# Attention and bilinear feed-forward on one core: the last out products as seven half products for eight

## The chip, the core and the metric

The kernel runs on one core of a Trainium2 chip: TensorE (matmuls into PSUM), VectorE, ScalarE, GpSimd (SBUF alone in this kernel), SyncE (SP), which issues most transfers, and 16 DMA engines. The metric is device time of one execution in microseconds; lower is better.

## The reference

Attention with a forget gate over 8 batches, 8 heads, 576 tokens and a head size of 64; its output, 4608 tokens of 512, goes through a bilinear feed-forward of 1536 features.

```python
scores = scale * np.matmul(q, k.transpose(0, 1, 3, 2))
log_f = np.log(np.clip(f, 0.0001, 1.0))
cum = np.cumsum(log_f, axis=-1)
decay = cum[:, :, :, None] - cum[:, :, None, :]
scores = np.where(causal, -1000000000.0, scores + decay)
attn = softmax(scores)
x = (attn @ v).transpose(0, 2, 1, 3).reshape(B * S, H * D)
out = ((x @ w_a) * (x @ w_b)) @ w_out
```

(softmax stands for the three lines that write it out.)

## The kernel before

Attention runs over 32 pairs of heads (pr, t). The feed-forward follows behind the batches that are ready: for a piece of 256 to 512 tokens (`cuts`) TensorE makes psa and psb, ScalarE copies psa to fp16 (a16), VectorE multiplies it by psb into the hidden tiles ht (line 1072), and the out step multiplies ht by w_out into pso, 12 feature blocks of 128 for each block of 128 tokens.

A product on TensorE is issued in two halves by `mm_halves` (line 74): 64 stationary columns each, on both halves of the array, over the same moving columns. The two run beside each other, and the text calls them a pair.

The last 1024 tokens are two halves of 512, which start at `TW` = (3584, 4096). Their hidden values come from `winograd`: x of the two halves and w_a, w_b are taken as 2 by 2 blocks, and for each of 12 feature blocks fb seven products (`product`, m 1 to 7, four matmuls of 512 columns each) stand for the eight plain ones. It needs differences of weights (`sub_w`, line 1218, named xT or wb after the buffers that they reuse) and of x (`add_x`, line 1224), fp16 on VectorE. The products gather in PSUM in wg and wb; `snap` copies stages of them to SBUF (wu, wv; ScalarE or VectorE), `combine` (line 1273) adds: c11, c12 and c22, and multiplies: h1 (first half's hidden values, on GpSimd, into hy or ht) and h2 (second half's, on VectorE, into hx). For odd fb c22 runs on GpSimd too (wv<-wv).

`out_step` then makes eight blocks of 128 tokens, 12 pairs of 512 columns each, a ScalarE copy to osb and a store by SP. The last block is cut into 256, 128 and 128 columns (`last_out`, `last_copy`, `last_store`: psz, half), and its middle piece is stored from ScalarE's queue.

What runs when is not decided at run time. Every step is an `Op` with dependencies; a planner outside the file laid them out, and its result stands in it as tables: ORDER (the sequence in which all Ops are issued), CHOICE (the engine, where there is one) and SLOTS (which buffer of each ring a tile gets). Each engine works through its own part of ORDER one instruction after another and waits at semaphores; a late instruction holds everything behind it on its engine.

```python
PLAIN = range(0, 12, 2)
for tb in range(8):
    out_step(TW[0], tb, muls[tb // 4], 0.04 * TW[0])
order = laid_out()
for o in order:
    o.fn(o.eng)
```

## Time and profile before

| | us |
|---|---|
| median of 3 runs | 396.08 |
| lowest, highest | 394.84, 400.15 |
| profiled execution, device time | 395.96 |
| its span, first to last instruction | 393.9 |

The busy shares by slice (40 slices of 9.85 us, tenths of busy time) show where each engine works:

```profile
PE   7899999999999999999999999999999989999997
DVE  7888898998997779788887798758998898989700
ACT  4998999999888878778988588789898662455221
POOL 8699677778877689884897779678976980357600
```

PE is TensorE, DVE VectorE, ACT ScalarE, POOL GpSimd. Attention and feed-forward share the slices up to the 33rd; the hidden stage of the last 1024 tokens fills slices 34 to 37, and their out step the last two.

### The profile page before, as it was taken

Reading aid. Unit: us, or ns where it says so; the run is one execution under the profiler, and the core shown is the slowest. Engines: PE = TensorE matmul, PEld = TensorE weight load, DVE = VectorE, ACT = ScalarE, POOL = GpSimd, SP = SyncE. Lnnn points to the kernel's source line nnn. Section 1 sums busy time; section 2 is a strip of 40 time slices with the busy share of each in tenths; the row PEclk is TensorE's granted clock in tenths of the full one; section 3 lists DMA queues with packets and bytes.
Section 4 is the critical chain, followed back from the end, with each engine's and each line's share of the span. In section 5 each row is a group of like instructions: output and inputs, shape, how many; then the busy total and the mean of one; then the engine's idle time right before and its main releaser. Section 6 shows DMA issues by size and latency. Waiting matters only on the chain.

```text
span 393.9 us, 14686 instructions
## 1 busy us (share of the span) xinstructions
PE 382.3 (97%) x5720; PEld 251.3 (64%) x5720; DVE 319.2 (81%) x1015; ACT 296.5 (75%) x817; POOL 280.4 (71%) x482
## 2 busy tenths in 40 slices
PE   7899999999999999999999999999999989999997
PEld 3557977969766665655555665555655677666665
DVE  7888898998997779788887798758998898989700
ACT  4998999999888878778988588789898662455221
POOL 8699677778877689884897779678976980357600
PEclk9999999999999999999999999999999999999999
DMA  7999999999999999999999999999999895100022
GB/s 125 265 188 173 153 147 232 231 289 284 188 233 245 219 285 211 263 236 266 256 229 264 256 227 213 260 270 229 207 203 223 185 139 137 55 1 2 2 108 107
DMA packets 147365, 76.87 MB, mean 195 GB/s; under 512 B 124384, under 2 KB 128352, under 8 KB 147296
## 3 DMA queue, kind: packets, MB, share of 16 engines
q1 hardware_dynamic: 132856, 68.72, 77.2%
q0 software_dynamic: 14256, 7.08, 14.6%
q8 instruction: 44, 0.72, 0.7%
q14 instruction: 25, 0.20, 0.2%
q10 hardware_dynamic: 184, 0.14, 0.1%
HBM read 52.05 MB, written 9.58 MB: 156 GB/s over the span
## 4 chain that ended last, share of the span: by engine, by line
PE 79%; DMA 7%; POOL 4%; DVE 4%; ACT 3%; issue 2%; DVEq 0%; ACTq 0%; POOLq 0%
PE pso L74 20%; PE psa L74 16%; PE psb L74 15%; PE wg L74 5%; PE wb L74 4%; PE sc L550 3%; PE pvx L768 3%; DMA PTB<-PB 2%; PE psT L358 2%; DMA wout<-in_moe_w_out_dram 2%; POOL PA L725 2%; PE sc L538 2%; ACT PA L704 2%; PE wake L74 2%; DVE S L673 2%
## 5 line engine op out<-in xcount | busy, mean ns | idle before, releaser
L673 DVE CUSTOM_DVE_ANT_0 S<-sc,spread 64x576 f32<-64x576 f32 (+4 forms) x232 | 125.4, 561 | 14.2 <-ACT PA L704 4.8
L725 POOL TENSOR_SCALAR PA<-PA,st 128x256 f16<-128x256 f16 (+2 forms) x180 | 85.6, 487 | 10.5 <-DVE st L714 7.5
L74 PE MATMUL psa<-xT,wa 128*64 128x512 f16 (+2 forms) x864 | 88.9, 333 | 1.7 <-DVE ht L1072 1.7
L74 PE MATMUL psb<-xT,wb 128*64 128x512 f16 (+2 forms) x864 | 88.7, 332 | 0.4 <-DVE ht L1072 0.2
L704 ACT ACTIVATE PA<-S,st 128x256 f16<-128x256 f32 (+2 forms) x168 | 84.1, 503 | 6.2 <-DVE st L673 5.7
L74 PE MATMUL pso<-wout,ht 128*64 128x512 f16 x696 | 85.5, 380 | 0.3 <-DMA wout<-in_moe_w_out_dram 0.3
L725 POOL TENSOR_SCALAR PB<-PB,st 128x512 f16<-128x512 f16 (+1 forms) x90 | 64.0, 719 | 23.4 <-DVE st L714 8.7
L74 PEld LDWEIGHTS <-wa 128*64 128x64 f16 x960 | 55.4, 110 | 26.3 <-issue 4.2
L74 PEld LDWEIGHTS <-wb 128*64 128x64 f16 x960 | 56.5, 110 | 24.3 <-issue 1.7
L288 ACT CAST a<-psa 128x512 f16<-128x512 f32 (+1 forms) x90 | 49.4, 551 | 18.1 <-PE psa L74 14.9
L1072 DVE TENSOR_TENSOR ht<-psb,a 128x512 f16<-128x512 f32 (+1 forms) x90 | 57.6, 649 | 6.2 <-PE psb L74 4.1
L74 PEld LDWEIGHTS <-ht 128*64 128x64 f16 x696 | 38.8, 110 | 27.9 <-issue 2.6
L704 ACT ACTIVATE PB<-S,st 128x512 f16<-128x512 f32 x56 | 40.2, 720 | 3.4 <-DVE st L673 2.9
L704 ACT ACTIVATION_READ_ACCUMULATOR PA<-S,st 128x1 f32 x168 | 31.9, 190 | 0.0
L700 ACT ACTIVATE PB<-S,st 128x576 f16<-128x576 f32 x28 | 21.7, 776 | 9.2 <-DMA PTB<-PB 3.6
L630 POOL TENSOR_SCALAR_AFFINE_SELECT spread<-spread 128x768 f32<-128x768 f32 x24 | 20.9, 871 | 10.7 <-DMA spread<-cum_d 10.3
L288 ACT COPY osb<-pso 128x512 f32<-128x512 f32 x28 | 16.3, 583 | 15.4 <-PE pso L74 15.4
L768 PEld LDWEIGHTS <-nv 128*64 128x64 f16 x640 | 22.0, 110 | 6.7 <-DMA PTA<-PA 2.1
L1273 POOL TENSOR_TENSOR hy<-wu 128x512 f16<-128x512 f32 x9 | 11.4, 1278 | 20.3 <-DVE wu L1273 20.3
L673 DVE CUSTOM_DVE_ANT_1 S<-sc,spread 128x256 f32<-128x256 f32 x48 | 19.7, 420 | 6.5 <-PE sc L538 1.9
L714 DVE RECIPROCAL st<-st 128x2 f32<-128x2 f32 x128 | 18.2, 156 | 7.4 <-ACT PA L704 3.8
L673 DVE DVE_READ_ACCUMULATOR2_ANT st<- 128x1 f32 (+1 forms) x280 | 22.9, 82 | 0.0
(136 smaller groups left out, 674.6 us busy)
## 6 DMA issues: line engine op xcount, KB each, us to landing
spread<-cum_d SPq DMA_DIRECT2D x24, 576.0 KB, 6.4
out_dram<-osb SPq DMA_DIRECT2D x35, 256.0 KB, 3.4
q<-in_q_dram SPq DMA_DIRECT2D x14, 576.0 KB, 5.3
k<-in_k_dram SPq DMA_DIRECT2D x14, 576.0 KB, 5.1
v<-in_v_dram SPq DMA_DIRECT2D x24, 256.0 KB, 6.0
wout<-in_moe_w_out_dram POOLq DMA_DIRECT2D x3, 512.0 KB, 8.0
nv<-in_v_dram POOLq DMA_DIRECT2D x8, 128.0 KB, 5.9
wa<-in_moe_w_a_dram POOLq DMA_DIRECT2D x2, 512.0 KB, 7.6
```

Of the source, the lines that this page charges most:

```text
L74: nc.tensor.matmul(out=out[r], lhsT=lhsT[:, r], rhs=rhs, **kw)
L288: nc.scalar.copy(out=out_, in_=in_)
L550: nc.tensor.matmul(out=dst, lhsT=lhsT, rhs=rhs, start=start, stop=stop, skip_group_check=True)
L630: nc.gpsimd.affine_select(out=c[:, :, 0:SM].rearrange("p h (j k) -> p h j k", k=128), in_=c[:, :, SM:2 * SM].rearrange("p h (j k) -> p h j ...
L673: nc.vector.tensor_tensor_reduce(out=o, in0=x, in1=y, scale=-1.0, scalar=3e38, op0=ADD, op1=MIN, accum_out=m)
L700: nc.scalar.activation(out=p_blocks(t, 4), in_=T[("s" if direct else "z", t, 4)], func=EXP, bias=st[:, 8:9], scale=sign, accum_out=st[:, 1 ...
L704: nc.scalar.activation(out=p_blocks(t, i)[:, :, h, :], in_=(T[("s", t, i)][:, h, :] if direct else T[("z", t, i)][:, h * n:h * n + n]).rea ...
L714: nc.vector.reciprocal(out=st[:, 20 + 2 * i:22 + 2 * i], in_=st[:, 10 + 2 * i:12 + 2 * i])
L725: VEC[e].tensor_scalar(out=p, in0=p, scalar1=st[:, c:c + 1], scalar2=1.0, op0=MUL, op1=MUL)
L768: nc.tensor.matmul(out=o[HP[h], 128 * i:128 * i + 128], lhsT=vt[:, j, pr + NP * h, :], rhs=pt[:, base_blk[i] + 2 * block_at(t, i, j) + h, ...
L1072: nc.vector.tensor_tensor(out=ht[:, 0:n_], in0=T.pop(("psb", t0, fbs))[:, 0:n_], in1=T.pop(("a16", t0, fbs))[:, 0:n_], op=MUL)
L1273: VEC[e].tensor_tensor(out=out_, in0=x, in1=y, op=op)
```

## The change

The out step of the last 1024 tokens is written as 2 by 2 blocks too: the two token halves; two halves of the 1536 features (`in_half`: blocks 0 to 2 and 6 to 8, and the rest); two halves of 256 of the 512 output columns. With H for hidden values, W for w_out:

- Weight differences (`sub_out`, tw0 to tw3, two VectorE operations of 768 columns each): T0 = W12 - W11, T1 = W22 - T0, T2 = W22 - W12, T3 = W21 - T1.
- Sums of hidden values (`add_h`, ten VectorE operations in fp16): S0 = H21 + H22, S1 = S0 - H11, S2 = H11 - H21 (over H21's place), S3 = H12 - S1. S0, S1 and S3 lie in the three spread buffers, which attention no longer needs. The planner is told that they follow all twelve h1 (`done`).
- Seven products for each of four block pairs (block p of both halves): m1 = H11 W11, m2 = H12 W21, m5 = S0 T0, m6 = S1 T1, m7 = S2 T2, m3 = S3 W22, m4 = H22 T3; six feature blocks, 256 columns. They run in phases over three groups of block pairs, (0, 1), (2) and (3). og gathers m1, m6, m7, m4; om gathers m5, m3; ob holds m2.
- For each group three snaps (of m1, m5, m1 + m6), three joins on VectorE (j11, j12, j22, line 1363 of the changed kernel), a ScalarE copy of og with m4, and two stores (three for the last group), all by SP.

Removed are the eight out blocks, their copies and stores. The number of instructions of the hidden products is unchanged. ORDER, CHOICE and SLOTS are new; what each engine issues is the same up to some 246 us and differs from there, in the last attention steps and feed-forward pieces as well. Of the tables the diff shows a line each.

```diff
-        568017a29bd345c0168279a34bd015c2;n16:011010010110001010010101010101;n32:0120102102102102010202121220120
...
+        8017a29bd345c0168279a35bd014c2;n16:01101001011000101001010101010110;n32:0120102102102102010202121220120
...
+    def in_half(k, f):
+        return 6 * (f // 3) + 3 * k + f % 3
+    def w_out(k, j, c):
+        return wout16.rearrange("p (a k f) c -> p a k f c", a=2, k=2)[:, j, k, :, 256 * c:256 * c + 256]
+    def sub_out(e, k, j):
+        if ("tw", k) not in T:
+            T[("tw", k)] = qkT_pool.tile([128, NP, S], FP16, tag=("qT", "kT")[k % 2], name="tw").rearrange(
+                "p a s -> p (a s)")[:, 0:1536].rearrange("p (f c) -> p f c", f=6)
+        t = lambda m: T[("tw", m)][:, 3 * j:3 * j + 3, :]
+        x, y = ((w_out, (0, j, 1)), (w_out, (1, j, 1)), (w_out, (1, j, 1)), (w_out, (1, j, 0)))[k], \
+            ((w_out, (0, j, 0)), (t, (0,)), (w_out, (0, j, 1)), (t, (1,)))[k]
+        VEC[e].tensor_tensor(out=t(k), in0=x[0](*x[1]), in1=y[0](*y[1]), op=SUB)
+    def hid(half, k, f, n=1):
+        x, fb = None, in_half(k, f)
+        if n == 1:
+            return T[("ht", TW[half], fb)]
+        return T[("hx" if half else "hy", fb // 3)].rearrange("p n k -> p (n k)")
+    def h_sum(k, f, n=1):
+        if k == 2:
+            return hid(1, 0, f, n)
+        if ("sh", k) not in T:
+            T[("sh", k)] = turn(("bc", ("sh", k)), "bc", spread).rearrange("p h s -> p (h s)").bitcast(FP16)
+        return T[("sh", k)][:, 512 * f:512 * f + 512 * n]
+    def add_h(e, k, f, n):
+        x, y = ((hid, (1, 0, f, n)), (h_sum, (0, f, n)), (hid, (0, 0, f, n)), (hid, (0, 1, f, n)))[k], \
+            ((hid, (1, 1, f, n)), (hid, (0, 0, f, n)), (hid, (1, 0, f, n)), (h_sum, (1, f, n)))[k]
+        VEC[e].tensor_tensor(out=h_sum(k, f, n), in0=x[0](*x[1]), in1=y[0](*y[1]), op=SUB if k else ADD)
+    GROUPS = ((0, 1), (2,), (3,))
+    def out_product(m, g):
+        if m == 1:
+            T[("og", g)] = ff_tile([128, 512], FP32, "og")
+        if m == 2:
+            T[("ob", g)] = slot(ps, [128, 2, 512], FP32, "sc", "ob")[:, 0, :]
+        if m == 5:
+            T[("om", g)] = ff_tile([128, 512], FP32, "om") if g == 2 else slot(ps, [128, 2, 512], FP32, "sc", "om")[:, 0, :]
+        for n, p in enumerate(GROUPS[g]):
+            o = T[({2: "ob", 5: "om", 3: "om"}.get(m, "og"), g)][:, 256 * n:256 * n + 256]
+            c = slice(128 * p, 128 * p + 128)
+            for f in range(6):
+                x = {1: lambda: hid(0, 0, f), 2: lambda: hid(0, 1, f), 3: lambda: h_sum(3, f), 4: lambda: hid(1, 1, f),
+                     5: lambda: h_sum(0, f), 6: lambda: h_sum(1, f), 7: lambda: h_sum(2, f)}[m]()[:, c]
+                w = {1: lambda: wout16[:, in_half(0, f), 0:256], 2: lambda: wout16[:, in_half(1, f), 0:256],
+                     3: lambda: wout16[:, in_half(1, f), 256:512], 4: lambda: T[("tw", 3)][:, f, :],
+                     5: lambda: T[("tw", 0)][:, f, :], 6: lambda: T[("tw", 1)][:, f, :],
+                     7: lambda: T[("tw", 2)][:, f, :]}[m]()
+                mm_halves(o, x, w, start=(f == 0 and n == 0 and m in (1, 2, 5)), stop=(f == 5), skip_group_check=True)
+    def o_buf(what, g):
+        if (what, g) not in T:
...
+            T[(what, g)] = x
+        return T[(what, g)]
+    def o_snap(e, m, g):
+        n = 256 * len(GROUPS[g])
+        x = o_buf("ov", g)[:, 0:n] if m == 5 else o_buf("ou", g)[:, 512 * (m == 6):512 * (m == 6) + n]
+        cast(e, x, T[("om" if m == 5 else "og", g)][:, 0:n], False)
+    def o_row(g, half, c, n=1):
+        k = len(GROUPS[g])
+        return o_buf(f"r{half}", g)[:, 0:512 * k].rearrange("p (k c) -> p k c", k=k)[:, :, 256 * c:256 * c + 256 * n]
+    def o_join(e, what, g):
+        n = 256 * len(GROUPS[g])
+        x, y, o = {11: lambda: ("ob", o_buf("ou", g)[:, 0:n], o_row(g, 0, 0)),
+                   12: lambda: ("om", o_buf("ou", g)[:, 512:512 + n], o_row(g, 0, 1)),
+                   22: lambda: ("og", o_buf("ov", g)[:, 0:n], o_row(g, 1, 1))}[what]()
+        x, y = (z.rearrange("p (k c) -> p k c", c=256) for z in (T[(x, g)][:, 0:n], y))
+        VEC[e].tensor_tensor(out=o, in0=x, in1=y, op=ADD)
+    def o_copy(e, g):
+        n = 256 * len(GROUPS[g])
+        cast(e, o_row(g, 1, 0), T[("og", g)][:, 0:n].rearrange("p (k c) -> p k c", c=256), False)
+    def o_store(e, g, half, c, n):
+        r0, k = TW[half] + 128 * GROUPS[g][0], len(GROUPS[g])
+        nc.sync.dma_start(out=out[r0:r0 + 128 * k, 256 * c:256 * c + 256 * n].rearrange("(k p) c -> p k c", p=128),
+                          in_=o_row(g, half, c, n))
+    def out_products(hids):
+        tws, shs, twu, shu = {}, {}, [None] * 4, {}
+        w_all = w_ops[("o", 0)] + w_ops[("o", 1)] + w_ops[("o", 2)]
+        for k in range(4):
+            for j in range(2):
+                o = tws[(k, j)] = Op("DVE", 0.54, lambda e, k=k, j=j: sub_out(e, k, j),
+                                     w_all + ([tws[(k - 1, j)]] if k == 1 else [tws[(1, j)]] if k == 3 else [])
+                                     + ([tws[(k, 0)]] if j else []), name=f"tw{k}")
...
+        done = [hids[(0, fb)][0] for fb in range(12)]
+        for k in (0, 1, 3, 2):
+            for f, n in ((0, 3), (3, 3)) if k != 3 else ((0, 3), (3, 1), (4, 1), (5, 1)):
+                use = [(half, in_half(kk, x)) for half, kk in {0: ((1, 0), (1, 1)), 1: ((0, 0),), 2: ((0, 0), (1, 0)), 3: ((0, 1),)}[k]
+                       for x in range(f, f + n)]
+                prev = [v for (kk, ff), v in shs.items() if kk == {0: -1, 1: 0, 2: 0, 3: 1}[k] and ff <= f < ff + 3]
+                o = Op("DVE", 0.41 if n == 1 else 0.95, lambda e, k=k, f=f, n=n: add_h(e, k, f, n),
+                       [hids[x][0] for x in use] + prev + done, name=f"sh{k}")
+                shs[(k, f)] = o
...
+        for g in range(3):
+            k_, n_ = len(GROUPS[g]), 256 * len(GROUPS[g])
+            pr_, sn = {}, {}
+            def mm(m, deps):
+                sums = {3: 3, 5: 0, 6: 1, 7: 2}
+                hs = {1: (0, 0), 2: (0, 1), 4: (1, 1), 7: (1, 0)}.get(m)
+                src = ([v for (k, f), v in shs.items() if k == sums[m]] if m in sums else []) + (
+                    [hids[(hs[0], in_half(hs[1], f))][0] for f in range(6)] if hs else [])
+                t = {4: 3, 5: 0, 6: 1, 7: 2}.get(m)
+                o = pr_[m] = Op("PE", 6 * n_ * COLS * 1.012, lambda _, m=m, g=g: out_product(m, g),
+                                [*src, *([tws[(t, 0)], tws[(t, 1)]] if t is not None else w_all), *deps], mode="full", name=f"vm{m}")
...
+                return o
+            def cp(m):
+                o = sn[m] = Op(None, {"ACT": 0.19 + 0.00078 * n_, "DVE": 0.15 + 0.00105 * n_}, lambda e, m=m, g=g: o_snap(e, m, g),
+                               [pr_[m]] + ([sn[1]] if m == 6 else []), name=f"osnap{m}")
+                return o
+            def join(what, deps):
+                return Op("DVE", 0.15 + 0.00105 * n_, lambda e, what=what, g=g: o_join(e, what, g), deps, name=f"oj{what}")
+            def store(half, c, n, deps):
+                return Op("SP", 0.53, lambda e, g=g, half=half, c=c, n=n: o_store(e, g, half, c, n), deps,
+                          land=packets(128 * k_, 1024 * n))
+            m1 = mm(1, [])
+            gu = take(m1, "ff")
+            s1 = cp(1)
+            uu = take(s1, "n32")
+            m2 = mm(2, [])
+            bu = take(m2, "sc")
+            j11 = join(11, [m2, s1])
+            au = take(j11, "S" if g < 2 else "nv")
+            bu.append(j11)
+            m5 = mm(5, [])
+            mu = take(m5, "ff" if g == 2 else "sc")
+            s5 = cp(5)
+            vu = take(s5, "n16" if g < 2 else "a16")
+            m6 = mm(6, [s1])
+            s6 = cp(6)
+            m3 = mm(3, [s5])
+            j12 = join(12, [m3, s6, j11])
+            mu.extend([s5, m3, j12])
+            au.extend([j12, store(0, 0, 2, [j11, j12])])
+            m7 = mm(7, [s6])
+            j22 = join(22, [m7, s5])
+            ru = take(j22, "osb" if g else "nv")
+            m4 = mm(4, [j22])
+            oc = Op("ACT", 0.19 + 0.00078 * n_, lambda e, g=g: o_copy(e, g), [m4, j22], name="ocp")
...
+            ru.append(oc)
+            ru.extend([store(1, 1, 1, [j22]), store(1, 0, 1, [oc])] if g == 2 else [store(1, 0, 2, [j22, oc])])
...
-        muls = [[], []]
-        hu = {}
+        hids, hu = {}, {}
...
-                muls[half].append((h, hu[key]))
-        for tb in range(8):
-            out_step(TW[0], tb, muls[tb // 4], 0.04 * TW[0])
+                hids[(half, fb)] = (h, hu[key])
+        out_products(hids)
...
-        2435 2438 2436 2437 2439-2446 2448-2450 2453 2451 2454 2447 2452 2455-2462
...
+        2425-2428 2474 2452 2436 2443 2475 2454 2439 2440 2478 2455 2456 2458 2457 2444 2445 2459 2441 2460
```

Three places in the order. First VectorE behind the last hidden product, before and after (h2 writes hx; spread1 is S0, spread2 S1, hx S2, spread0 S3; r0, nv and osb are output rows; the square brackets name the engines or DMA queues waited for):

```order
L1273 TENSOR_TENSOR wu_8662<-wb_8653,wu_8662 128x512 [waits DVE_49,PE_49]
L1273 TENSOR_TENSOR wv_8677<-wv_8677,wg_8607 128x512 [waits PE_49]
L1273 TENSOR_TENSOR hx_8647<-wg_8607,wv_8677 128x512 [waits DVE_49,PE_49]
L1273 TENSOR_TENSOR hx_8647<-wg_8626,wv_8670 128x512 [waits Pool_49]
L292 COPY osb_8997<-psz_8972 128x128 [waits DMAHW3_49,DMAHW5_49,DMAHW1_49,DMAHW7_49,PE_49,Activation_49]
```

After, from the last h2 on:

```order
L1273 TENSOR_TENSOR hx_8663<-wg_8617,wv_8701 128x512 [waits Pool_49]
L1307 TENSOR_TENSOR spread1_85<-hx_8322,hx_8442 128x1536
L1307 TENSOR_TENSOR spread1_85<-hx_8567,hx_8663 128x1536 [waits DVE_49]
L1363 TENSOR_TENSOR r0_8840<-ob_8786,ou_8769 128x2x256 [waits PE_49,Activation_49]
L1363 TENSOR_TENSOR r0_8857<-ob_8812,ou_8855 128x256 [waits PE_49,Activation_49]
L1307 TENSOR_TENSOR spread2_86<-spread1_85,hy_8299 128x1536 [waits DVE_49]
L1307 TENSOR_TENSOR spread2_86<-spread1_85,hy_8605 128x1536 [waits DVE_49]
L1307 TENSOR_TENSOR hx_8567<-hy_8605,hx_8567 128x1536
L1307 TENSOR_TENSOR hx_8322<-hy_8299,hx_8322 128x1536
L1307 TENSOR_TENSOR spread0_84<-hy_8370,spread2_86 128x1536 [waits DVE_49]
L1307 TENSOR_TENSOR spread0_84<-ht_8653,spread2_86 128x512 [waits DVE_49]
L1307 TENSOR_TENSOR spread0_84<-ht_8698,spread2_86 128x512
```

Where VectorE had one copy left, it now has a chain of sums, joins and a snap. Second, VectorE inside the hidden stage, where a difference stands among the combinations; before, the last third of w_b's own difference:

```order
L1273 TENSOR_TENSOR wu_8357<-wb_8338,wu_8357 128x512 [waits Activation_49]
L1273 TENSOR_TENSOR hx_8303<-wg_8242,wv_8325 128x512 [waits DVE_49,PE_49]
L1218 TENSOR_TENSOR wb16_77<-wb16_77 128x2x512
L292 COPY wv_8397<-wb_8378 128x512 [waits DVE_49,PE_49]
L1273 TENSOR_TENSOR wu_8366<-wb_8378,wu_8366 128x512 [waits Activation_49]
```

After, both parts of T3 (a third tw, T2's second part, stands nearer to the stage's start):

```order
L1273 TENSOR_TENSOR hx_8442<-wg_8379,wv_8455 128x512 [waits DVE_49,PE_49]
L1273 TENSOR_TENSOR wu_8471<-wb_8473,wu_8471 128x512 [waits Activation_49]
L1289 TENSOR_TENSOR tw_8527<-wout16_78,tw_8034 128x768 x2
L1273 TENSOR_TENSOR wv_8511<-wv_8511,wg_8457 128x512 [waits DVE_49]
L1273 TENSOR_TENSOR wu_8505<-wb_8514,wu_8505 128x512 [waits Activation_49]
```

All three parts of w_b's difference moved ahead of the stage. Third, SP's last stores, before and after:

```order
L1118 DMA out_0_dram<-osb_8866 128x512 [waits DMAHW2_49,Activation_49]
L1118 DMA out_0_dram<-osb_8885 128x512 [waits DMAHW3_49,Activation_49]
L1118 DMA out_0_dram<-osb_8913 128x512 [waits DMAHW4_49,Activation_49]
L1114 DMA out_0_dram<-half_8949 128x256 [waits DMAHW5_49,Activation_49]
L1114 DMA out_0_dram<-osb_8997 128x128 [waits DMAHW7_49,DVE_49]
```

After:

```order
L1371 DMA out_0_dram<-r0_8840 128x2x512 [waits DMAHW0_49]
L1371 DMA out_0_dram<-nv0_79 128x2x512 [waits DMASW6_49,DMASW7_49,DMASW1_49,DMAHW1_49,DMASW0_49,Activation_49]
L1371 DMA out_0_dram<-osb_9065 128x512 [waits DMAHW2_49,Activation_49]
L1371 DMA out_0_dram<-osb_8985 128x256 [waits DMAHW3_49,Activation_49]
L1371 DMA out_0_dram<-nv1_80 128x512 [waits DMASW6_49,DMAHW4_49,DMASW2_49,DVE_49]
```

The last store is one of 128x512 values behind a join on VectorE, where it was one of 128x128 behind a copy. TensorE's last products run, by group: m4 of the first and second, m2 of the third, m4 of the third, m3 of the third.

80 lines of the change are left out of this document (57 added, 23 removed), and 58 rows, old and new, of the table ORDER.

## The prediction

> **What bounds the kernel now.** I read the page's busy shares and slices first, then a table by stage, then who TensorE waited for, and last the chain of work that ended last.
>
> ```profile
> span 393.9 us, 14686 instructions
> PE 382.3 (97%) x5720; PEld 251.3 (64%) x5720; DVE 319.2 (81%) x1015; ACT 296.5 (75%) x817; POOL 280.4 (71%) x482
> 246.00:332.70 86.70, 84.91 (x1223) 52.38 (x1221) 72.15 (x240) 64.87 (x184) 62.20 (x114) 1.00 0.97 208
> 332.70:371.75 39.05, 39.05 (x364) 25.84 (x362) 34.95 (x58) 18.66 (x34) 21.23 (x17) 1.00 0.06 22
> 371.75:391.02 19.27, 19.25 (x226) 13.41 (x222) 1.38 (x2) 4.74 (x9) 1.44 (x2) 1.00 0.26 97
> 391.02:393.90 2.88, 0.00 (x0) 0.00 (x0) 0.29 (x1) 0.00 (x0) 0.00 (x0) 1.00 0.27 84
> PE psa L74 <- DVE ht L1072: 1.7, 1, 1.7
> ```
>
> The four rows of stages give start and end, length, and then busy time of TensorE, its weight loads, VectorE, ScalarE and GpSimd, the granted clock, the DMA share and GB/s. TensorE is busy without a gap from 332.7 to 391.02 at the full clock; in the 86.7 us ahead of that it lost 1.8 us, nearly all in one wait for VectorE (last row). So what the change takes from TensorE's columns comes off the end, as long as VectorE delivers; in the hidden stage (332.70 to 371.75) VectorE is busy for 34.95 of 39.05 us. Up to 246 us both kernels issue the same work in the same order, and I count nothing there.
>
> ```profile
> 370.22 0.86 PE pso L74 x8
> 371.95 16.40 PE pso L74 x152
> 388.35 2.67 PE psz L74 x72
> 391.09 0.29 DVE osb L292
> ```
>
> The chain of waits ends in TensorE's out products alone, one VectorE copy of 128x128 and a store. The profiled execution took 395.96 us, 2.06 more than its span, and stands 0.12 under the median of the runs shown (396.08); I sum against 395.96.
>
> **The out step.** It leaves TensorE with 96 pairs of 512 columns (two matmuls of 64 output rows run beside each other as a pair) and gets 7 products x 4 block pairs x 6 feature blocks = 168 pairs of 256. From the chain, 152 matmuls or 76 pairs of 512 took 16.40 us: 0.2158 each. The psz piece, 12 pairs of 256 and 24 of 128, took 2.67. The two equations (512r + c = 0.2158; 6144r + 36c = 2.67) give r = 0.415 ns a column and c = 3.3 ns a pair, so 256 columns cost 0.1095 us. Before: 84 x 0.2158 + 2.67 = 20.8; after: 168 x 0.1095 = 18.4. Saved: **2.4 us**.
>
> Each weight load now serves half the columns, 336 loads for 192. I cost that at nothing: the psz stretch fed pairs of 128 columns, and its pace is in the 2.67.
>
> ```profile
> L74 PE MATMUL psz<-wout,hx 128*64 128x128 f16 x48 | 1.5, 219 | 0.0
> L74 PE MATMUL psz<-wout,hx 128*64 128x256 f16 x24 | 1.5, 273 | 0.0
> L288 ACT COPY half<-psz 128x256 f32<-128x256 f32 x1 | 0.4, 373 | 0.7 <-PE psz L74 0.7
> ```
>
> **The eight weight differences** (tw, 768 fp16 columns on VectorE). Nearest rows are the same operation at 1024 and 512 columns:
>
> ```profile
> L1218 DVE TENSOR_TENSOR xT<-wb,wa x3: 680/868/873, 289.6 to 324.8; 128x1024 f16<-128x1024 f16 x3
> L1218 DVE TENSOR_TENSOR xT<-wb,xT x3: 677/680/2925, 313.1 to 330.6; 128x1024 f16<-128x1024 f16 x3
> L1218 DVE TENSOR_TENSOR wb<-wb x3: 676/681/682, 326.1 to 346.3; 128x1024 f16<-128x1024 f16 x3
> L1218 DVE TENSOR_TENSOR xT<-wa,xT x3: 682/683/691, 327.4 to 334.0; 128x1024 f16<-128x1024 f16 x3
> L1224 DVE TENSOR_TENSOR xT<-xT,xT x5: 414/416/425, 331.8 to 336.6; 128x512 f16<-128x512 f16 x5
> ```
>
> Between 0.415 and 0.68 lies 0.55 for 768, in all 4.4 us. Four of the eight (with all three wb differences, of which two come forward out of the hidden stage) stand where GpSimd was idle for 13.94 us, ahead of its first hidden product. There TensorE has its last pso blocks to run: all earlier pso work now stands ahead of the first hidden product, one 0.86 us piece more of cover. One stands among the ht products, three inside the hidden stage. Cover in all three places is TensorE's own queue; if it is gone, the next ht slot (then psa) or the next c11 and c12 (then the products m3 and m4) is late. The maximum of 2925 ns above is what happens when such an operation meets GpSimd:
>
> ```profile
> 310.94 1.39 POOL L725 TENSOR_SCALAR PA<-PA,st 128x256 f16<-128x256 f16 x3
> 312.86 1.27 POOL L725 TENSOR_SCALAR PA<-PA,st 128x384 f16<-128x384 f16 x3
> 313.06 2.92 DVE L1218 TENSOR_TENSOR xT<-wb,xT 128x1024 f16<-128x1024 f16 x1
> 314.09 0.40 POOL L637 TENSOR_SCALAR_AFFINE_SELECT spread<-spread 128x256 f32<-128x256 f32 x1
> 315.41 0.92 POOL L725 TENSOR_SCALAR PA<-PA,st 128x256 f16<-128x256 f16 x1
> 316.63 0.84 PE L74 MATMUL psa<-xT,wa 128*64 128x384 f16 x8 [1.73 <-DVE ht L1072]
> 339.09 1.27 POOL L1273 TENSOR_TENSOR hy<-wu 128x512 f16<-128x512 f32 x1 [13.94 <-DVE wu L1273]
> ```
>
> A 0.68 us difference took 2.92 beside a run of GpSimd instructions, and TensorE lost 1.73 behind it. The GpSimd row at 315.41 took 0.92, where three like it took 1.39 together: the two hold each other up. Of the twelve L1218 three were stretched, by 0.19, 0.19 and 2.24. I take the same loss for the new order as for the old, so **0** in the difference, with ends of -1.7 (it does not recur) and +1.7 (once more).
>
> [...]
>
> **The hidden stage.** Fewer pso pieces lie inside it: 0.86 near its start and 0.86 twice near its end before, now 6 pairs of 256 (0.66) near its end.
>
> ```profile
> 335.96:373.92 37.96, 37.96 (x355) 25.11 (x353) 33.41 (x53) 17.55 (x32) 22.67 (x18) 1.00 0.04 16
> 371.92 1.27 POOL L1273 TENSOR_TENSOR wv<-wv 128x512 f32<-128x512 f32 x1
> 373.23 0.69 DVE L1273 TENSOR_TENSOR hx<-wg,wv 128x512 f16<-128x512 f32 x1 [0.55 <-POOL wv L1273]
> ```
>
> From its first c11 to its last h2 VectorE worked 33.41 of 37.96 us. Its window shrinks by 3 x 0.86 - 0.66 = 1.9, and its work changes by 3 x 0.55 (tw) less one copy and one wb difference (0.68 each), +0.3. Of 4.55 us idle 2.3 are left. The cost is 0 if the idle time was slack and 2.2 if it was all needed; following products and snaps by hand over the stage's first ten I meet no new wait, so I take **+0.2**.
>
> **The sums behind it.** Call 371.75, the end of the last hidden product, t. In the old run VectorE ended its last h2 2.17 after t, held by GpSimd's wv row, which was last there. In the new order GpSimd makes that wv one place earlier and ht last, so by hand 1.7. Behind it stand ten sums: seven of 1536 columns (0.68 + 0.265 = 0.945 each, continued from 512 and 1024) and three of 512 (0.415), and between them joins and a snap that read PSUM (0.69 for 512 columns as in the last row, 0.42 for 256 between that and the 0.29 copy of 128). TensorE meanwhile has m1 for the two groups still open and m2 for two: 36 pairs, 3.9 us. m5 needs the first sums at t + 3.9 and has them at 1.7 + 2 x 0.945 = 3.6. m6 begins at 6.6; its sums are there by 3.6 + 0.69 + 0.42 + 1.9 = 6.6. m3 begins at 11.2, after m6 and two groups of m7; it needs seven sums, two joins, three small sums and the om snap: 1.7 + 6.6 + 1.1 + 1.25 + 0.69 = 11.35. So TensorE waits 0.2, or 0.6 with 2.17 for 1.7; overlap of one operation's start with the last one's end (33.41 us for 53 operations of mostly 0.69 is 0.63 each) takes some of that back. I take **+0.3**, ends 0 and 2. GpSimd ends at about 1.7 too, so the sums meet nothing there. ScalarE's eleven copies behind the hidden stage need under 6 us of some 17.
>
> **The end.** Before: copy 0.29, a 64 KB store. After: a 256-wide join, 0.42 (+0.13), and a 256 KB store, behind one of 512 KB, one of 256 and one of 128 on SP (ScalarE's queue issues none any more).
>
> ```profile
> DMA to landing us min/median/max: 2.0/3.4/6.0
> out_dram<-half SPq DMA_DIRECT2D x1, 128.0 KB, 1.7
> out_dram<-osb SPq DMA_DIRECT2D x1, 64.0 KB, 1.6
> ```
>
> The first row is of the 256 KB stores at L1118, most beside loads and transposes; the tail has neither. Bounds +0.4 and +1.8; I take **+0.6**, near the minimum, since the DMA share in the last stages was 0.26; the groups' joins come late, though, so all 2 MB now leave in some 6.6 us, and the 512 KB store is issued 2.4 us ahead of the last one, which leaves it time.
>
> **Sum:** -2.4 + 0.2 + 0.3 + 0.13 + 0.6 = **-1.2 us**. Span 392.7, device time **394.8**.
>
> **Rivals.** (1) The loss of 1.73 at 314 does not recur, since the differences fall elsewhere against GpSimd: 393.1. For it: nine of twelve were not stretched. Against: six such operations now stand between the ht products, where three stood. (2) The fp16 differences meet GpSimd. The three in the hidden stage can each wait for a product of 1.27 us: 3.8 us on VectorE against 2.3 of idle time left, so TensorE is held for 1.5, and the time is 396.3, no change; a second event like that at 313 gives 396.5. [...] For it: GpSimd was busy for 21.23 of 39.05 us in that stage. Against: the wb difference that stood among the old products was not stretched, and nor were eight others. (3) The slower side: VectorE ends the hidden stage late, and the sums become the bound. The place is m5 and m3, the price one us for each us, and it decides once the last h2 ends 3.2 after t, which eats the gain. If VectorE needs all its old idle time (2.2 not there), it ends at 3.9, and TensorE waits 2.4 where I count 0.5: 396.7, slower than before by 0.7. For it: 35 of 39 us busy. Against: ScalarE is half idle there. (4) The products shorten, but the end does not move, since the stores set it: at 3.4 to 4 us to landing it is 1.2 to 1.8 later, 396.0 to 396.6, no change. For it: 2 MB in 6.6 us are some 320 GB/s, where the last stage had 97. Against: the minimum of 2.0 for 256 KB and 1.6 for 64, which make 0.4 us for 192 KB, or 2 MB in 4.3.
>
> **Chances.** Forecast 0.42, (1) 0.17, (2) 0.17, (3) 0.13, (4) 0.11. The range takes in (1) and (2), (3) and (4) with a run's spread on both sides, 392.4 to 397.6. Most of that is a gain or no change; the forecast's own range is 393.9 to 395.7. A measurement tells this kernel from no change at about 2%, 7.9 us: faster would be under 388.2 and no case reaches it (0.02); slower would be over 404.0, and needs several of the losses together (0.03).
>
> **What would show it.** Right: in the new trace the vm products take 0.11 us a pair, TensorE has no gap over 0.3 us between the last hidden product and its end, and that stretch lasts some 18 us; the tw rows stay near 0.55, and the last store lands about 2.2 us after its issue. Wrong: tw rows of over 1 us with a wait of TensorE behind them; a gap at the first m5 or m3 that VectorE ends; a span that ends more than 4 us after TensorE; a weight load that holds the pairs at over 0.11; or a new wait between 246 and 332 us, where the whole order was made anew and I count nothing.

## The result and the profile after

| | old kernel | new kernel |
|---|---|---|
| median, us | 395.53 (6 runs, 393.84 to 400.15) | 400.31 (6 runs, 398.14 to 401.44) |
| span of the profiled execution, us | 393.9 | 398.7 |

The new kernel takes 1.0119 times as long (95% interval 1.0086 to 1.0152), 4.7 us more (3.4 to 6.0). I forecast 1.2 us less. That 1.2% is under the 2% that I had named as what a measurement can tell, but the interval leaves no change out.

The new kernel's page, busy time and share of each engine, and the slices of TensorE, VectorE and GpSimd:

```profile
span 398.7 us, 14905 instructions
PE 381.5 (96%) x5816; PEld 254.9 (64%) x5816; DVE 335.9 (84%) x1043; ACT 296.8 (74%) x818; POOL 284.0 (71%) x482
...
PE   7899999999999999989999999999998897999996
...
DVE  7888898998997779787888797889776997998892
...
POOL 8699677769877689884996877858857784266600
```

TensorE's busy time fell (382.3 to 381.5) and the span grew: the loss is mostly waiting. It shows in slices 31, 32 and 34, which have 8, 8 and 7, where the old kernel has nines (its one 8 there is the 33rd): ahead of the hidden stage, not in the rewritten out step. The table by stage (start, end, length, then busy time of TensorE, weight loads, VectorE, ScalarE, GpSimd, granted clock, DMA share, GB/s) says the same:

```profile
246.00:340.00 94.00, 88.44 (x1248) 54.44 (x1244) 79.15 (x253) 65.43 (x185) 66.78 (x116) 1.00 0.93 200
340.00:377.31 37.31, 37.31 (x352) 24.10 (x350) 33.70 (x57) 19.84 (x36) 21.33 (x17) 1.00 0.04 16
377.31:395.01 17.70, 17.68 (x324) 17.41 (x320) 13.38 (x22) 4.27 (x10) 1.41 (x2) 1.00 0.21 77
395.01:398.70 3.69, 0.00 (x0) 0.00 (x0) 0.42 (x1) 0.00 (x0) 0.00 (x0) 1.00 0.56 210
```

Behind 340.00 TensorE has no gap. Ahead of it 5.56 of 94 us are idle, where the old kernel had 1.8 in its 86.7. Whom TensorE waited for in that stretch (total, times, longest; pvx is the attention product, PTA and PTB are what a DMA writes transposed for it, sc is a score product, L673 VectorE's scan of the scores):

```profile
PE pvx L768 <- DMA PTA<-PA: 1.6, 1, 1.6
PE sc L550 <- DVE st L673: 1.4, 1, 1.4
PE psb L74 <- DVE st L673: 1.1, 1, 1.1
PE pvx L768 <- DMA PTB<-PB: 0.9, 1, 0.9
```

So the loss has two places. The two waits for scans, 2.5 us together, lie in slices 31 and 32; VectorE and TensorE there:

```profile
307.45 0.42 DVE L673 CUSTOM_DVE_ANT_1 S<-sc,spread 128x256 f32<-128x256 f32 x1 [1.78 <-POOL spread L630]
307.94 0.84 PE L74 MATMUL psb<-xT,wb 128*64 128x384 f16 x8 [1.14 <-DVE st L673]
311.39 2.33 DVE L1218 TENSOR_TENSOR xT<-wb,wa 128x1024 f16<-128x1024 f16 x1
315.23 0.39 PE L550 MATMUL sc<-kT,qT 64*128 64x512 f16 x2 [1.40 <-DVE st L673]
```

The first scan waited for GpSimd's spread, which itself had waited 1.65 us for a DMA. The second stood behind a weight difference of the hidden stage that took 2.33 us, for 0.68 when alone, while GpSimd worked: the same kind of loss as the old kernel's 1.73. The two waits for transposes, 2.5 us, lie in slice 34, ahead of the hidden stage.

The chain of waits up to the hidden stage shows where these come from (start, length, what it was):

```profile
323.39 3.55 POOL PB L725 x3
...
329.10 1.83 POOL PA L725 x2
330.93 2.59 POOL PB L725 x2
333.52 0.02 issue
333.54 3.95 DMA PTB<-PB
...
338.27 1.73 PE pso L74 x16
340.00 0.86 PE wg L74 x8
```

GpSimd's last normalisations (L725) end at 333.52, their transpose lands at 337.49, the last attention product follows and then one out block. In the old kernel GpSimd was done at 325.15 and TensorE had out blocks to run until 332.7, so the chain did not matter.

The two executions cannot be compared by absolute times. A VectorE scan that both issue at the same place in the same order stands at

```profile
246.44 0.76 DVE L673 CUSTOM_DVE_ANT_0 S<-sc,spread 64x576 f32<-64x576 f32 x1
```

in the old kernel and at 247.78 in the new one; over all the profiles of this study it moved between 245.67 and 250.27, with the same order of work ahead of it. I call its start m and count from it:

| from m, us | old | new |
|---|---|---|
| GpSimd's last normalisation ends | 78.71 | 85.73 |
| first hidden product | 86.46 | 92.02 |
| length of the hidden stage | 39.05 | 37.51 |
| from its end to the span's end | 21.95 | 21.39 |
| all | 147.46 | 150.92 |

The two lines above the last hold the rewritten part. One out block piece of 0.86 moved from the hidden stage to ahead of it. So the hidden and out steps gained 1.54 + 0.56 - 0.86 = 1.24, and the stretch ahead of them lost 5.56 - 0.86 = 4.70. Of that, 3.77 is idle time (5.56 us from m to the first hidden product, for 1.79); the other 0.93 stands as busy time of TensorE, with no matmul more than the piece that moved (1228 for 1220). A matmul ahead of a wait still counts as busy for the length of its record, in the old trace 0.195 us for 64 columns and 0.38 for 512, and the new kernel has six waits for the old one's one; that may be most of it, and is not shown. From m this pair of executions differs by 3.46, and the medians by 4.7: that the stretch's 4.70 equals this last figure is chance.

The ratios, here and below, leave out slow executions, those over 1.5% above the fastest of their kernel; the medians do not, and the profiled one of e6 is such a one, with its loss ahead of m (250.17).

### The profile page after: what moved, and what is told of

The parts are those of the page before. It is cut to its first block, busy times and chain, and to the rows that moved or that the text cites. A ratio compares the mean times of both kernels' runs of the same rounds, so it can differ in the third digit from the quotient of the medians.

```text
span 398.7 us, 14905 instructions
## 1 busy us (share of the span) xinstructions
PE 381.5 (96%) x5816; PEld 254.9 (64%) x5816; DVE 335.9 (84%) x1043; ACT 296.8 (74%) x818; POOL 284.0 (71%) x482
## 5 line engine op out<-in xcount | busy, mean ns | idle before, releaser
L673 DVE CUSTOM_DVE_ANT_0 S<-sc,spread 64x576 f32<-64x576 f32 (+4 forms) x232 | 125.5, 562 | 12.7 <-ACT PA L704 2.8
L725 POOL TENSOR_SCALAR PA<-PA,st 128x256 f16<-128x256 f16 (+2 forms) x180 | 86.5, 490 | 8.8 <-DVE st L714 4.5
L725 POOL TENSOR_SCALAR PB<-PB,st 128x512 f16<-128x512 f16 (+1 forms) x90 | 65.9, 738 | 24.9 <-ACT osb L288 8.3
L74 PE MATMUL pso<-wout,ht 128*64 128x512 f16 x672 | 82.3, 380 | 0.2 <-DVE ht L1072 0.2
L673 DVE CUSTOM_DVE_ANT_1 S<-sc,spread 128x256 f32<-128x256 f32 x48 | 19.7, 420 | 9.4 <-POOL spread L630 3.8
L550 PE MATMUL sc<-kT,qT 64*128 64x512 f16 (+4 forms) x144 | 21.0, 326 | 2.6 <-DVE st L673 1.4
L673 DVE DVE_READ_ACCUMULATOR2_ANT st<- 128x1 f32 (+1 forms) x280 | 22.9, 82 | 0.0
```

Source lines behind the costliest of these rows:

```text
L74: nc.tensor.matmul(out=out[r], lhsT=lhsT[:, r], rhs=rhs, **kw)
L550: nc.tensor.matmul(out=dst, lhsT=lhsT, rhs=rhs, start=start, stop=stop, skip_group_check=True)
L673: nc.vector.tensor_tensor_reduce(out=o, in0=x, in1=y, scale=-1.0, scalar=3e38, op0=ADD, op1=MIN, accum_out=m)
L725: VEC[e].tensor_scalar(out=p, in0=p, scalar1=st[:, c:c + 1], scalar2=1.0, op0=MUL, op1=MUL)
```

## Experiments

Twelve kernels, each run beside the old one. The last three columns of the table are of one profiled execution each; what they give for the difference to the old kernel agrees with the ratio within 1.5 us in every row. A number in the order table is one operation: 2413 and 2414 are the halves of tw0, then tw1 (2415, 2416), tw2 (2417, 2418) and tw3 (2419, 2420). "Old order" means the old kernel's order, engines and buffers up to and through the hidden stage, with the new out step behind it.

| | ratio to the old kernel (95%) | first hidden product from m | hidden stage | all from m |
|---|---|---|---|---|
| new kernel | 1.0119 (1.0086 to 1.0152) | 92.02 | 37.51 | 150.92 |
| e1 old order, differences in the hidden stage | 1.0080 (1.0060 to 1.0101) | 86.34 | 42.70 | 150.38 |
| e2 old order, five early | 1.0084 (1.0051 to 1.0116) | 88.06 | 41.48 | 150.91 |
| e3 new order, differences in the hidden stage | 1.0176 (1.0145 to 1.0207) | 94.43 | 39.73 | 155.46 |
| e4 new order, old out step | 1.0154 (1.0115 to 1.0194) | 93.42 | 38.47 | 154.26 |
| e5 old order, none | 0.9957 (0.9920 to 0.9995) | 86.21 | 38.98 | 146.55 |
| e6 old order, in gaps | 0.9982 (0.9948 to 1.0016) | 85.50 | 39.94 | 146.83 |
| e7 new order, wait for GpSimd | 1.0152 (1.0106 to 1.0198) | 88.55 | 45.03 | 154.92 |
| e8 e7 and GpSimd's queue | 1.0166 (1.0122 to 1.0209) | 88.69 | 44.03 | 154.03 |
| e9 e8 mended | 1.0069 (1.0041 to 1.0096) | 88.24 | 40.20 | 149.77 |
| e10 as e6, four on GpSimd | 1.0009 (0.9973 to 1.0046) | 85.10 | 41.12 | 147.53 |
| e11 new order, none | 1.0148 (1.0102 to 1.0194) | 94.32 | 37.67 | 153.34 |
| e12 as e6, in one gap | 0.9938 (0.9906 to 0.9969) | 85.69 | 38.75 | 145.79 |

### The order or the differences: e1 to e4

I began with two theories: A, the remade order loses the time by itself; B, the early weight differences hold up GpSimd.

e1 (old order; one difference behind each of eight h2 of the hidden stage):

```diff
-... 2193 2413 2415 2194 ...
+... 2257 2413 2266 ...
+... 2288 2414 2300 ...
```

> Edit: the new out step (seven half products, sums, stores) behind the old kernel's order of everything up to and through the hidden stage; all eight weight differences are put one by one into the hidden stage. Theory A (the remade order of the attention's last third, 246 to 332 us in the old run, loses the time whatever is put into it): about 1 us under the old kernel, as my sum had it, so near 394.5 where the old one gives 395.5. Theory B (the five early weight differences, fp16 with two SBUF inputs, hold up GpSimd's last normalisations): also near 394.5, since none of them stands there any more. Theory C (the out step itself costs more than my sum): 398 to 400. A loss of 0.5 to 1.5 from eight differences in the hidden stage's full VectorE would fit A and B both.

It came to 399.23 us beside 396.04, where both theories had 394.5. That is what the third, C, had, but from the end of the hidden stage to the span's end e1 took 21.34 us for the old kernel's 21.95, so the out step is not what costs; the hidden stage is. The tw rows (min, median, max in ns):

```profile
L1289 DVE TENSOR_TENSOR tw<-wout x4: 548/780/1075, 345.8 to 362.3; 128x768 f16<-128x768 f16 x4
L1289 DVE TENSOR_TENSOR tw<-wout,tw x4: 541/869/1245, 348.0 to 369.4; 128x768 f16<-128x768 f16 x4
```

The longest of them on VectorE's timeline, and the GpSimd product that it met on GpSimd's:

```profile
365.66 1.25 DVE L1289 TENSOR_TENSOR tw<-wout,tw 128x768 f16<-128x768 f16 x1
```

```profile
365.22 1.27 POOL L1273 TENSOR_TENSOR hy<-wu 128x512 f16<-128x512 f32 x1 [2.29 <-DVE wu L1273]
```

Whom TensorE waited for in that hidden stage:

```profile
PE wb L74 <- DVE wu L1273: 1.3, 4, 0.4
PE wg L74 <- DVE wv L1273: 1.0, 1, 1.0
```

A difference took 0.54 us at best; the four that took 1.01 to 1.25 all began inside a GpSimd product. VectorE is busy for 40.0 of 42.8 us and TensorE waits behind it. The hidden stage is full: eight differences made it 3.7 us longer.

e2 (old order; 2417 among the last scans, 2413 to 2416 around VectorE's last reciprocal, three in the hidden stage):

```diff
+... 1700 2413 2415 1574 ...
+... 2213 2414 2416 2194 ...
```

> Edit: as the run before it, but five of the weight differences stand where the new kernel has them: one among the last scans, four behind VectorE's last reciprocal, while GpSimd still normalises. Theory A: the same as the run before it within 0.5 us, near 394.5, because the old order has some 8 us of out blocks on TensorE behind the last attention product to cover it. Theory B: 2 to 4 us more than the run before it, 396.5 to 398.5, with rows of GpSimd's normalisations again stretched from 0.69 to over 1.2 us.

399.59 us: the hidden stage began 1.7 later than in e1, as B had it in kind, and was still 2.4 longer than the old kernel's, which neither had; one of the three differences in it took 1.6 us (the longest row of tw). The kernel took 0.4 us more than e1 where B had 2 to 4. In the old order, e1's places and e2's both made the kernel some 3 us slower than the old one.

e3 (new order; 2413 to 2418 each behind an h2 of the hidden stage):

```diff
-... 2193 2413 2415 2194 ...
+... 2257 2413 2256 ...
```

> Edit: the new kernel, its order kept, with the six weight differences that stood ahead of or at the start of the hidden stage put one by one into the hidden stage. Theory A: no change against the new kernel, 399.5 to 400.5 (about 4.5 above the old one). Theory B: 2 to 4 us under the new kernel, 396.5 to 398, GpSimd's last normalisation ending about 331 instead of 333.5 in the profile and the waits of the last pvx for PTA and PTB (2.5 us together) mostly gone.

403.06 us, slower than the new kernel. The attention's end did not come earlier (last normalisation 85.90 from m, for 85.73) and the hidden stage grew by 2.2. B falls for the new order.

e4 (new order; old out step, no weight differences):

```diff
-        out_products(hids)
+        for tb in range(8):
+            out_step(TW[0], tb, muls[tb // 4], 0.04 * TW[0])
```

> Edit: the new kernel's order of everything up to and through the hidden stage, with the old out step (24 full products) behind it and no weight differences of the out step at all. Theory A: slower than the old kernel by 4.5 to 6.5 us, 400 to 402, since the order's loss is there and the out step's gain of about 1 is not. Theory B: the old kernel's time to 2 us above it, 395.5 to 397.5.

402.73 us, just above A's 400 to 402. The new order alone carries the loss; but e1 and e2 show that the differences have a price of their own, which A denied.

### What the out step is worth: e5 and e11

Products 4 to 7 read stored weights, so no difference is needed. e5 does it in the old order, e11 in the new kernel:

```diff
-        VEC[e].tensor_tensor(out=t(k), in0=x[0](*x[1]), in1=y[0](*y[1]), op=SUB)
+        return
...
-                     5: lambda: T[("tw", 0)][:, f, :], 6: lambda: T[("tw", 1)][:, f, :],
+                     5: lambda: w_out(0, 1, 0)[:, f % 3, :], 6: lambda: w_out(0, 0, 1)[:, f % 3, :],
```

> Edit: as e1 (the old kernel's order up to and through the hidden stage, the new out step behind it), but the eight weight differences of the out step are left out: products 4, 5, 6 and 7 read slices of the stored out weights in their place, of the same size, so the output is not the reference's. Theory D (the eight differences are the price, wherever they stand: VectorE had no free room for them, and each either holds up GpSimd and the attention, or TensorE in the hidden stage): 0.5 to 1.5 us under the old kernel, 394.5 to 395.5 where the old one gives 396.0, as my sum had it for the out step. Theory C (the out step's products, sums and stores cost more than my sum): as e1, 398 to 399.5.

> Edit: the new kernel with the eight weight differences of the out step left out (products 4 to 7 read stored out weights of the same size, so the output is not the reference's); its order of everything else is kept. If the order of the rest loses the time by itself, as e4 said: 399.5 to 401.5. If the differences lose it in this order: 396 to 398.

e5 is 0.43% under the old kernel, 1.7 us (0.2 to 3.2); the medians of all its executions and the old kernel's, 395.60 and 396.18, lie 0.6 apart, and from m it is 0.9 less. So the out step without its differences is worth about what the sum said, 1.2. e11 has the same operations as e5, with another order and another engine for some copies, and is 1.9% slower. Its GpSimd rows:

```profile
323.32 3.55 POOL L725 TENSOR_SCALAR PB<-PB,st 128x512 f16<-128x512 f16 x3
...
329.05 2.65 POOL L725 TENSOR_SCALAR PA<-PA,st 128x128 f16<-128x128 f16 x2
331.67 1.79 POOL L725 TENSOR_SCALAR PB<-PB,st 128x512 f16<-128x512 f16 x2
```

And two stretches around the end of the attention, in the columns of the table by stage:

```profile
338.00:340.00 2.00, 2.00 (x32) 1.39 (x33) 0.51 (x2) 0.64 (x1) 0.00 (x0) 0.60 0.03 9
340.00:342.00 2.00, 2.00 (x14) 1.04 (x11) 1.90 (x6) 0.00 (x0) 0.00 (x0) 0.55 0.00 0
```

The normalisations are stretched without any tw: the hidden stage's own fp16 differences (L1218) come forward and meet GpSimd instead; the one at 328.45 took 1.15 us, for 0.68 when alone. Then TensorE, which waited 1.9 and 1.1 us for the transposes, ran on at 0.60 and 0.55 of its clock for four us, and lost 1.7 by it, as I estimate from the clock (2 x 0.40 + 2 x 0.45); its out block of 16 matmuls took 3.52 us there, for 1.92 in the new kernel. The profiled execution of the new kernel, with 1.6 and 0.9 of waiting, kept its clock at 1.00; two of its other five show a mean of 0.996, as do some of e11's. The 1.7 is most of the 2.4 us by which e11's execution is slower from m than the new kernel's, although it does less; over all executions the two ratios overlap. In e3 and e4 too the clock averaged 0.98 from m to the first hidden product, as in e11.

### What in the new order: e7 to e9

e7 puts twelve fp16 differences (eight of the hidden stage's and four tw, which began between 323 and 335 us) behind a copy of one column that GpSimd's last normalisation writes:

```diff
+        if (k, c.start) == (1, 1024):
+            nc.vector.tensor_copy(out=after_norm, in_=p_blocks(BH // 2 - 1, 3)[:, 0, 1, 0:1])
         VEC[e].tensor_tensor(out=b[:, 0:2] if out_ is None else out_[:, :, c], in0=x, in1=y, op=SUB)
```

> Edit: the new kernel, its order kept but for VectorE's fp16 differences from 323 us on (eight of the hidden stage's weights, four of the out step's), which stand behind a one-column copy that waits for GpSimd's last normalisation: they can no longer run beside one. If the stretched normalisations (7.98 us in the new kernel's profile from 323.39 on for seven instructions that take 4.1 unhindered) are what makes the attention late: GpSimd ends 3 to 4 us earlier and the kernel gains 1.5 to 3.5 us, 397 to 399. If the lateness comes from the order alone: 400 to 402, since VectorE's work only starts later.

Its GpSimd rows (line numbers are one higher):

```profile
323.11 2.09 POOL L726 TENSOR_SCALAR PB<-PB,st 128x512 f16<-128x512 f16 x3
...
327.35 0.74 POOL L726 TENSOR_SCALAR PA<-PA,st 128x128 f16<-128x128 f16 x2
328.05 1.39 POOL L726 TENSOR_SCALAR PB<-PB,st 128x512 f16<-128x512 f16 x2
```

And TensorE's longest wait from 246 us on:

```profile
PE wb L74 <- DVE xT L1227: 4.4, 1, 4.4
```

The same seven normalisations take 4.2 us where they took 7.98 in the new kernel; GpSimd ends 4.2 earlier from m and the hidden stage begins 3.5 earlier. So the stretching is real and lay on the path. But the kernel gained nothing (402.61): VectorE's work now came late, and TensorE waited 4.4 us for the sums of its second products and then ran some six us at half its clock (the rows are in the last section), which by my estimate (4.4 and half of six) together make about the 7.5 us by which the hidden stage is longer than the new kernel's. What it is in the two engines that collides no run shows; the price, 7.98 against 4.2 us, is what this pair of traces shows.

e8 adds a change of GpSimd's queue (1621 and 1665 are the masks that waited for VectorE):

```diff
-... 1516 1530 1680 1621 ...
+... 1516 1530 1680 1557 1558 1639 1621 ...
-... 1594 1665 ...
+... 1594 1528 1665 ...
```

> Edit: as e7, and on GpSimd three normalisations stand ahead of the spread's masking at 315.25 us, which waited 2.08 us for VectorE's scans, and one cast ahead of the one at 321.46, which waited 1.75: work that was ready goes first. If head-of-queue waits on GpSimd are the second part of the loss: 0.5 to 2 us under e7. If the chain is held by the scans themselves (VectorE) and GpSimd has slack: as e7 within 0.5.

402.56 us, and from m the same end of GpSimd (81.53 for 81.56). Taking the waits from the head of GpSimd's queue gained nothing. In e7 and e8 VectorE had stood idle ahead of its differences, for over 3 us of it with GpSimd already done, behind a copy of an out block that TensorE had yet to compute (e8):

```profile
330.55 0.69 DVE L293 COPY osb<-pso 128x512 f32<-128x512 f32 x1 [4.88 <-PE pso L74]
```

e9 moves that copy (2200) behind eight of the twelve:

```diff
-... 2199 2200 2202 ... 2213 2414 ...
+... 2199 2202 ... 2213 2200 2414 ...
```

> Edit: as e8, with one copy of an out block on VectorE (which waited 4.88 us for TensorE ahead of the differences in e8, while GpSimd had long ended) moved behind eight of the differences. Theory E (in the new order two things lose the time: VectorE's fp16 differences beside GpSimd's last normalisations, and work that is ready queued on GpSimd behind a waiting instruction; e7 and e8 cured both, and paid it back in the 4.4 to 4.6 us for which TensorE waited for the hidden stage's sums): 4 to 6 us under e8, 396.5 to 398.5, a start of the hidden stage near 334.5 and a wait under 1 us behind it. If the hidden stage's sums come no earlier, because VectorE is simply full there: 400 to 402.

398.66 us, 1% under e8 and a little above what I expected; two waits of 1.2 us for VectorE stay at the start of the hidden stage. It is 0.5% better than the new kernel, with intervals that just overlap. The first hidden product is still 1.8 us later from m than in the old order, although nothing stretches GpSimd's last normalisations any more. The out block piece that moved is 0.86 of that. Another 0.7 is idle time of TensorE, 2.5 us from m to the hidden stage for the old kernel's 1.8, and nearly all of it is the two waits for scans, which stay:

```profile
306.68 0.84 PE L74 MATMUL psb<-xT,wb 128*64 128x384 f16 x8 [1.01 <-DVE st L674]
314.02 0.39 PE L551 MATMUL sc<-kT,qT 64*128 64x512 f16 x2 [1.45 <-DVE st L674]
```

Both waits stand in every trace of the new order: 0.9 to 1.9 us the first, 1.40 to 1.46 the second. No experiment took them away, so what they are worth is read from the traces and not shown by a run.

### Differences that fit: e6, e10, e12

> Edit: as e1, with the eight differences put where the old kernel's trace shows an engine idle: two at 301.5 us, where GpSimd stands idle (VectorE), two at 306.4 in a gap of 1.28 us of VectorE, two at 328.6 in a gap of 1.30, and the last two on GpSimd in the hidden stage, where it is busy for 21.5 of 39.3 us. Theory D: each still costs something, but less: the old kernel's time to 2 us above it, 396 to 398. If only the place matters and those gaps are free: as e5, 394.5 to 395.5. Theory C: 398 to 399.5.

> Edit: as e6 (old order, new out step, differences spread), with the pair that stood ahead of the hidden stage on VectorE moved to GpSimd in the hidden stage too: four differences on GpSimd there (1.66 us each), four on VectorE at 301 to 307 us. If GpSimd has that room (21.5 busy of 39.3 us, and 6.6 more): as e5, 394 to 395, 1 to 2 us under the old kernel. If its products come late and TensorE waits for them: 396 to 397.5.

> Edit: as e6, with the second of its two differences on GpSimd put right behind the first, in the stretch of 3.77 us in which GpSimd stands idle in the profile of e5 (351.9 to 355.7); in e6 the second delayed GpSimd's chain from 359 us on and TensorE waited 0.94 us at 364.0. If the price of the differences is only what they collide with: e5's time, 0.3 to 0.6 per cent under the old kernel (394.5 to 395.5 where that gives 396.3), with no wait of TensorE over 0.4 us in the hidden stage. If each difference costs wherever it stands: as e6, 0.1 to 0.3 per cent under the old kernel.

All three keep the old order. They put 2413 to 2416 on VectorE where the old trace shows VectorE or GpSimd idle. e6 and e12 put 2417 and 2418 into VectorE's gap at 328.6 and 2419 and 2420 on GpSimd; e10 puts all four on GpSimd:

```diff
-                o = tws[(k, j)] = Op("DVE", 0.54, lambda e, k=k, j=j: sub_out(e, k, j),
+                o = tws[(k, j)] = Op("POOL" if k == 3 else "DVE", 0.54, lambda e, k=k, j=j: sub_out(e, k, j),
...
-... 2302 2419 2298 ... 2318 2420 2339 ...
+... 2302 2419 2420 2298 ...
```

e10 has `k > 1` in place of `k == 3`. The first pair of lines is e6's and e12's; the second leads from e6 to e12. GpSimd's timeline in e6 (idle time ahead of a row in brackets):

```profile
354.14 1.66 POOL L1289 TENSOR_TENSOR tw<-wout,tw 128x768 f16<-128x768 f16 x1
357.99 1.28 POOL L1273 TENSOR_TENSOR hy<-wu 128x512 f16<-128x512 f32 x1 [2.19 <-DVE wu L1273]
359.22 1.65 POOL L1289 TENSOR_TENSOR tw<-wout,tw 128x768 f16<-128x768 f16 x1
```

TensorE's gap behind it:

```profile
364.00 0.62 PE L74 MATMUL wg<-xT,xT 128*64 128x512 f16 x4 [0.94 <-ACT wu L288]
```

And GpSimd in e12:

```profile
352.79 3.25 POOL L1289 TENSOR_TENSOR tw<-wout,tw 128x768 f16<-128x768 f16 x2
356.60 1.28 POOL L1273 TENSOR_TENSOR hy<-wu 128x512 f16<-128x512 f32 x1 [0.57 <-DVE wu L1273]
```

In e6 the first fits into a gap and the second does not; TensorE pays 0.94, and e6's 394.76 us cannot be told from the old kernel's 396.18 (the interval holds 1). e12 puts both into the gap, and GpSimd still waits 0.57 for VectorE behind them, so they delay nothing. e12 took 394.36 us beside 396.71, 0.62% under the old kernel (0.31 to 0.94), and about 1.8% under the new one: 2.5 us better than the old kernel with the same operations that made the new one 4.7 worse. From m it is 1.7 faster. Not all of that was planned. In e6, e10 and e12 the old kernel's wait of 1.73 ahead of the hidden stage is gone (e1 and e5 still have 1.6 and 1.5): up to there the only change is the early tw, so I take them to have shifted VectorE's later work, and the stretched weight difference no longer held TensorE. From m to the first hidden product TensorE is idle for 0.6 us in e12, 1.6 in e5 and 1.8 in the old kernel. So e12 beside e5 does not show that a well placed difference is free: what the eight cost is offset by what this saved. e10 overfilled GpSimd (two waits of 1 us), came to 397.34 us beside 396.28 and gained nothing.

## Why the prediction was wrong

- **The step that failed** is the term that the sum does not have: "between 246 and 332 us, where the whole order was made anew and I count nothing". (That nothing differs up to 246 us holds.) That term is +4.7 us from m. e4 and e11 show that the order alone carries it, with no weight difference in the program. The traces put 2.5 of it on the last transposes, late because GpSimd's last normalisations were stretched to 7.98 us; e7, without the stretching, began the hidden stage 3.5 earlier. The two waits for scans are 2.5 more, in place of the old kernel's one wait of 1.73; no run takes these away, so their part is read from the traces alone.
- **The eight differences at 0**: the cover that I named, "where GpSimd was idle for 13.94 us" with "its last pso blocks" on TensorE, was read off the old execution. In the new one GpSimd normalised until 333.5 and one out block was left, so four of them ran beside its last normalisations. In this order they are not what costs: without them the hidden stage's own differences collide (e11). In the old order their price runs from 0 (e12 beside e5) to some 5 us (e1 beside e5, 1.0080 against 0.9957). That 0 includes the old wait that went away in e12. My ends of -1.7 and +1.7 were too near. The one loss beside GpSimd that I carried over unchanged, 1.73, came back as 1.40.
- **Out-step columns, -2.4**: 324 matmuls in 17.68 us, 0.1091 a pair for 0.1095 predicted. Right, and the weight loads hid, though they were busy for 17.41 of the 17.70 us. The 192 loads that I gave the old out step are 240, since the psz pieces have one for each of their 72 matmuls; the page's count grows by 96, as 336 for 240 has it.
- **Hidden stage +0.2, sums +0.3, end +0.73**: the planner's three differences in the hidden stage stayed at 0.55 us and TensorE was never idle there. But by the pieces that left it the stage should have shrunk by 1.9 and shrank by 1.54, so some 0.4 went in late starts too short to show as idle time, for +0.2. Behind it TensorE lost 0.02 us, for +0.3; the end took 3.69 for 2.88, +0.81. Hidden and out step together gained 1.24, where the sum had 1.2: the terms were near, and that they meet so closely is luck.
- **Rivals**: (2) named the right mechanism, fp16 differences beside GpSimd, in the wrong places (the hidden stage, or one more event like that at 313) and too small. (1), (3) and (4) did not happen, though what (1) describes came about in e6, e10 and e12. The last part named "a new wait between 246 and 332 us" as what would prove me wrong, without a chance or a price.

## What to carry to other kernels

When an order is made anew, the work that it moves is part of the change: take the last item of each chain that must end before the rewritten stage (here GpSimd's last normalisation and its transpose), and count in the new order what TensorE has left to cover it. An engine's idle stretch in the old trace is room only if the order around it stays; here the old order with eight operations put by hand into gaps that its trace showed beat both kernels, in part because a wait went away that nobody had aimed at. Compare traces from an instruction that both issue in the same place, since such an instruction came up to 4.6 us later in one execution than in another, with the same work ahead of it.

## What the hardware showed besides

- TensorE's granted clock fell in e7, and the loss outlasted the wait. Behind the 4.4 us, which ended at 342.35, it averaged 0.50 from 342 to 348 us:

```profile
339.00:342.00 3.00, 0.00 (x0) 0.00 (x0) 3.00 (x7) 0.00 (x0) 0.00 (x0) 0.91 0.16 61
342.00:345.00 3.00, 2.65 (x12) 1.26 (x12) 2.85 (x7) 1.07 (x2) 0.00 (x0) 0.50 0.00 0
345.00:348.00 3.00, 3.00 (x18) 1.59 (x17) 2.22 (x4) 0.73 (x2) 0.00 (x0) 0.50 0.00 0
348.00:351.00 3.00, 3.00 (x30) 1.88 (x28) 2.03 (x4) 1.84 (x4) 1.28 (x1) 0.95 0.02 5
```

  From 342.35 on each group of four matmuls of 512 columns took 1.06 to 1.11 us, for 0.62 to 0.63 at the clock of 1.00. All six executions of e7 show a mean clock of 0.991 to 0.995. In e11 it averaged 0.60 and 0.55 in the two stretches behind waits of 1.9 and 1.1 us, between which TensorE worked. What sets the clock no run shows.
- A weight difference of 768 fp16 columns took 0.55 us on VectorE (median of the four tw<-wout in e12) and 1.64 to 1.66 on GpSimd (e12, e6).
